# Float64 weights to float32 in three vector operations instead of four, early low parts on VectorE, early v read where it was loaded

## Chip, core and metric

The kernel runs on one core of a Trainium2 chip. The metric is the device time of one execution in microseconds (us). PE is TensorE, DVE VectorE, ACT ScalarE, POOL GpSimd and SP the engine whose queue issues the DMAs.

## What is computed

Banded attention feeds a gated two-layer network, and that feeds a second one; everything is float32, but the six weight matrices arrive as float64.

```
scores = q @ k.T / 8 - slope_h * distance        # 4 batches, 8 heads, 768 positions, 64 wide
a      = softmax(scores where key < n_global or 0 <= query - key < n_local)
x      = a @ v                                    # as [3072, 512]
h      = x @ w_in                                 # [512, 2048]
x2     = (h * clip(h + 3, 0, 6) / 6) @ w_out      # [2048, 512]
out    = ((x2 @ w1) * (x2 @ w2)) @ w3 @ w_out2    # 1024 wide inside
```

## The kernel before

**Matmuls.** Large products are made from operands in two parts: a high part, rounded to the matmul's shorter format by a ScalarE copy, and a low part, the rest. Each product is three matmuls (high by high, low by high, high by low), recorded by `mm3` (line 64). The 3072 tokens go in eight tiles of 384.

**Weights.** 72 pieces of [128, 512] float64 are brought in one after another (`w_issue`, SP, three buffers `st`). Each goes through `w_abs` (line 148, ACT: absolute value of the upper words), `w_f32` (lines 161, 163, 165, 167: four DVE operations that shift and join the two words' bits into a float32, tile `cvt`), and then `w_split`: high part on ACT (line 171), low part on POOL (line 172). `w_steps` deals this work out in ticks, four to a piece. In tick 1 the piece before is split and the first of the four operations stands; ticks 2 to 4 hold the other three, and tick 4 also `w_abs` of the next piece and the load of a later one.

**Attention.** 32 units (two heads, half of a batch's queries), of three blocks of 128 queries; a loop of 96 steps and three to drain runs over the blocks in a software pipeline. One step, s, holds the scores of block s (PE, line 424), its maximum (DVE, line 434) and exponential (ACT, line 443); the normalising of block s - 1 (two small DVE operations, lines 449 and 450, and a POOL multiplication, line 451); the transposes and copy of block s - 2 (PE line 459, ACT); and the product with v of block s - 3 (PE line 490), whose two parts ACT and DVE write as `xt` (lines 356 and 359). The score tiles have one buffer each, so that the next block's scores on PE wait for this block's maximum on DVE. The first eight units (`WHOLE`) use full float32 matmuls, and `prep_v` copies their v on ACT (line 347) from the loaded tile `rv` into `vh`.

**Where the weights meet it.** From step 4 on each step holds four ticks, thus one piece of weights: 16 pieces (half of w_in and w_out) are converted in about steps 5 to 20. From step 14 on the matmuls of the first network fill PE between the attention's. After the attention the other half of w_in and w_out (16 pieces) is wanted at once, dealt out by ticks after each 850 or 600 ns of matmul work; the remaining 40 pieces follow in the course of that stage.

**What sets the order.** Every engine runs its instructions in the order in which this program writes them down; nothing is reordered later. `psm` has three PSUM buffers for the products `h` and `x`; DVE (line 528) or ACT (line 582) must have read one before PE writes it again.

```
nc.vector.scalar_tensor_tensor(t, a, TINY, hi, ALU.is_ge, ALU.mult)                              # 161
nc.vector.tensor_scalar(au, tu, 5, 2, ALU.logical_shift_left, ALU.logical_shift_right)           # 163
nc.vector.scalar_tensor_tensor(au, lo, 29, au, ALU.logical_shift_right, ALU.bitwise_or)          # 165
nc.vector.scalar_tensor_tensor(tu, tu, 0xC0000000, au, ALU.bitwise_and, ALU.bitwise_or)          # 167
```

Of the kernel before, what the change touches and what calls it, by code (L numbers as in the profile page):

```python
# [20 lines left out]
# A float64's upper word, read as a float32, is at least this from 2**-126 on.  # L21
TINY = float.fromhex("0x1.2p-15")


class Filler:
    """Queued matmul work, run in pieces between the steps of something else."""
# [28 lines left out]
def mm3(nc, out, jobs, ns, every=4, hook=None, first=True, last=True):  # L55
    """out = (or out +=) sum of a.T @ b; each job holds ((a_hi, a_lo), (b_hi, b_lo)). The hook runs before the fourth
    from last."""
    n = len(jobs)
    done = 0
    for i, ((ah, al), (bh, bl)) in enumerate(jobs):  # L60
        if hook is not None and i == max(0, n - 4):
            hook()
        for j, (a, b) in enumerate(((ah, bh), (al, bh), (ah, bl))):
            nc.tensor.matmul(out, a, b, start=(first and i == 0 and j == 0), stop=(last and i == n - 1 and j == 2))  # L64
            done += 1
            if done % every == 0:
                yield every * ns
    if done % every:
        yield (done % every) * ns
# [3 lines left out]
def kernel(ctx: ExitStack, tc: tile.TileContext, q, k, v, n_global, n_local,  # L73
# [50 lines left out]
    def need(*keys):  # L124
        """Ends when what the keys stand for has been emitted."""
# [4 lines left out]
    def w_issue(src):  # L130
        """src: float64 bits (or float32) as [128, n] or [128, a, n / a]."""
# [11 lines left out]
    def w_abs(x):  # L143
# [4 lines left out]
        nc.scalar.activation(a, st.bitcast(F32).rearrange("p (c t) -> p c t", t=2)[:, :, 1], AF.Abs)  # L148
        return a

    def w_f32(x, a):
        """float32 of what was loaded: the upper 24 bits of a float64's significand."""
# [4 lines left out]
        lo = st.rearrange("p (c t) -> p c t", t=2)[:, :, 0]  # L157
        hi = st.bitcast(F32).rearrange("p (c t) -> p c t", t=2)[:, :, 1]
        t = cvp.tile([P, 512], F32, tag="cvt", name="cvt", bufs=2)
        au, tu = a.bitcast(U32), t.bitcast(U32)  # L160
        nc.vector.scalar_tensor_tensor(t, a, TINY, hi, ALU.is_ge, ALU.mult)  # L161
        yield t
        nc.vector.tensor_scalar(au, tu, 5, 2, ALU.logical_shift_left, ALU.logical_shift_right)  # L163
        yield t
        nc.vector.scalar_tensor_tensor(au, lo, 29, au, ALU.logical_shift_right, ALU.bitwise_or)  # L165
        yield t
        nc.vector.scalar_tensor_tensor(tu, tu, 0xC0000000, au, ALU.bitwise_and, ALU.bitwise_or)
        yield t

    def w_split(t, hi, lo):  # L170
        nc.scalar.activation(hi, t, AF.Copy)  # L171
        nc.gpsimd.tensor_tensor(lo, t, hi.bitcast(F32), ALU.subtract)  # L172

    def w_steps():
        """Splitting one, bringing the next to float32, loading a third, in four pieces."""
        while True:
# [20 lines left out]
            if conv is not None:  # L197
                next(conv)
            if wload and not wload[0][2]:
                wload[0][2].append(w_abs(wload[0][0]))  # L200
# [34 lines left out]
    def load_unit(i):  # L235
# [22 lines left out]
        vr = att.tile([P, 2 * HB, 2, D], F32, tag="rv", name="rv")  # L258
# [33 lines left out]
    def masks(mk):  # L292
        """What is added to q k / slope: minus the distance, or -BIG (and the rest) for a key that is not kept."""
# [29 lines left out]
    def out_of_band():  # L323
        """How many of the two counts' bounds (of the banded path) fail."""
# [11 lines left out]
    def new_prep(i):  # L336
        def two(tag, shape):
            return tuple(att.tile(shape, F32R, tag=tag + z, name=tag + z) for z in "hl")
        prep[i] = dict(q=two("q", [P, HB * P]), k=two("k", [P, 2 * HB, P]), v=two("v", [P, 2 * HB, 2 * D]))

    def prep_v(i):
        hf = units[i][1]
        nv = 2 * HB - 1 + hf
        r = raw[i][3].rearrange("p n j d -> p n (j d)")[:, :nv]
        vh, vl = (x[:, :nv] for x in prep[i]["v"])
        if i < WHOLE:
            nc.scalar.activation(vh.bitcast(F32), r, AF.Copy)
            return
# [121 lines left out]
    def a_pv(st):  # L470
# [3 lines left out]
        vh, vl = prep[i]["v"]  # L474
# [6 lines left out]
        for j in range(2):  # L481
            jobs = []
            for t in range(nk):
                a, al = (x[:, c0 + t, j * D:(j + 1) * D] for x in (vh, vl))
                if i < WHOLE:
                    jobs.append((a.bitcast(F32), ph[:, t, j, :].bitcast(F32)))
                else:
                    jobs += [(a, ph[:, t, j, :]), (al, ph[:, t, j, :]), (a, pl[:, t, j, :])]
# [19 lines left out]
    def parts(x, g):  # L508
        """The two parts of x, at the next call (or flush)."""
# [13 lines left out]
    def gate(h, g):  # L523
        """g = h * min(max(h + 3, 0), 6)."""
# [18 lines left out]
    def first(t, WI, f0):  # L543
        """h and g of one tile of tokens."""
# [8 lines left out]
    def second(t, WO, done, f0):  # L553
        """Sums of g's products with w_out, each given to done."""
# [122 lines left out]

    for f in range(FB):
# [13 lines left out]
    def gen_w34():  # L692
        """w3 @ w_out2, one block of 128 rows after another."""
# [39 lines left out]
    def step(gen, ns):  # L733
        """All of gen, with a pump and other work after each ns of it."""
# [87 lines left out]
def general_path(tc, ident, c3, nbits, slope, q, k, v, weights, out):  # L822
# [5 lines left out]
    with tc.tile_pool(name="gdr", bufs=1, space=DRAM) as dr:  # L828
# [4 lines left out]
        with tc.tile_pool(name="gc", bufs=1) as gc, tc.tile_pool(name="gw", bufs=2) as gw, \  # L833
# [6 lines left out]
            # float64 to float32, as long runs of any shape  # L840
# [22 lines left out]
            # the counts as float32: upper word * 2**32 + lower word without sign  # L863
# [11 lines left out]
            # distances and masks of each block of 128 queries  # L875
# [157 lines left out]
```

## Time and profile before

| | |
|---|---|
| median of 3 runs | 1286.88 us (1286.28 to 1287.11) |
| span of the profiled execution | 1286.8 us |
| PE busy | 1238.0 us, 96% |
| DVE busy | 611.0 us, 47% |
| ACT busy | 564.8 us, 44% |
| POOL busy | 466.5 us, 36% |
| mean granted TensorE clock | 0.982 of 2.4 GHz |

The profiled execution's span is its own time as far as it is given; it lies 0.1 us from the median, so nothing of size stands around it. The shares are averages over stages that have different limits, so the table by stages (rows 1 below) is to be read before it. Busy time of PE is modelled, since matmuls are pipelined.

### The profile page before, as it was taken

The numbers are of one execution on the slowest core, as the hardware profiler recorded it, in microseconds if no ns is written. First come the engines' busy times: TensorE is split into PE (matmuls) and PEld (weight loads), VectorE is DVE, ScalarE is ACT, GpSimd is POOL, SyncE is SP. The second block draws the span as 40 slices with busy tenths as digits, with TensorE's granted clock in tenths as the row PEclk, the third lists the DMA queues.
The fourth block names the chain that finished last, engine by engine and source line by source line (L and its number), as shares of the span: only waits on it lengthen the run. The fifth ranks groups of instructions, "written<-read, shape, count | busy, mean of one in ns | idle before, by whom it ended". The sixth has DMA issues, their size and how long they took to land. (4 is left out here: it accounts for less than half of the span.)

```text
span 1286.8 us, 20618 instructions
## 1 busy us (share of the span) xinstructions
PE 1238.0 (96%) x7512; PEld 1134.0 (88%) x7512; DVE 611.0 (47%) x1523; ACT 564.8 (44%) x1441; POOL 466.5 (36%) x417
## 2 busy tenths in 40 slices
PE   6789999999999999879999999999999999999997
PEld 4567898999898989769999999999899898998996
DVE  5998566666666664989644446731010010010100
ACT  6777566666666664445324234442222222222221
POOL 2555354444445352556203034554322222222210
PEclk9699999999999999989999999999999999999999
DMA  6662424242324302545444345433201001010000
GB/s 159 160 187 62 123 58 132 60 127 74 103 67 120 79 2 91 164 174 168 158 159 144 115 135 176 142 99 106 68 8 50 23 28 49 17 33 31 9 17 28
DMA packets 164624, 119.16 MB, mean 93 GB/s; under 512 B 109217, under 2 KB 154273, under 8 KB 164513
## 3 DMA queue, kind: packets, MB, share of 16 engines
q1 hardware_dynamic: 164224, 117.74, 31.0%
q8 instruction: 62, 1.02, 0.3%
q14 instruction: 50, 0.40, 0.1%
q10 hardware_dynamic: 288, 0.00, 0.0%
HBM read 87.30 MB, written 30.41 MB: 91 GB/s over the span
## 5 line engine op out<-in xcount | busy, mean ns | idle before, releaser
L793 DVE TENSOR_TENSOR abr<-abr,pb 128x384 f32<-128x384 f32 x64 | 35.5, 554 | 349.0 <-PE pb L64 349.0
L451 POOL TENSOR_TENSOR e<-e,su 128x512 f32<-128x512 f32 (+1 forms) x96 | 93.0, 969 | 167.1 <-DVE su L450 160.4
L528 DVE SCALAR_TENSOR_TENSOR t<-t,h 128x384 f32<-128x384 f32 x128 | 70.6, 551 | 114.4 <-ACT t L527 114.0
L443 ACT ACTIVATE e<-e,mx 128x256 f32<-128x256 f32 (+1 forms) x192 | 92.7, 488 | 58.9 <-DVE mx L434 58.5
L527 ACT ACTIVATE t<-h,c 128x384 f32<-128x384 f32 x128 | 73.3, 573 | 41.4 <-PE h L64 40.5
L172 POOL TENSOR_TENSOR wa<-cvt,wa 128x512 fp32r<-128x512 f32 x40 | 61.8, 1545 | 64.2 <-ACT wa L171 58.5
L490 PE MATMUL pv<-ph,vh 128*64 128x128 f32 x440 | 79.8, 260 | 4.5 <-DVE xt1l L359 4.0
L148 ACT ACTIVATE cva<-st 128x512 f32<-128x512 f32 x72 | 47.9, 666 | 68.6 <-DMA st<-in_moe_w_dram 48.6
L434 DVE CUSTOM_DVE_ANT_0 e<-s,base 128x256 f32<-128x256 f32 (+1 forms) x192 | 69.1, 397 | 12.0 <-PE s L424 10.9
L64 PE MATMUL h<-xt0h,wa 128*128 128x384 f32 x256 | 74.4, 357 | 0.0
L64 PE MATMUL h<-xt1h,r 128*128 128x384 f32 x256 | 67.3, 343 | 5.9 <-DVE t L528 3.1
L64 PE MATMUL h<-xt1h,wa 128*128 128x384 f32 x256 | 71.5, 349 | 1.4 <-DVE t L528 1.4
L165 DVE SCALAR_TENSOR_TENSOR cva<-st,cva 128x512 uint32<-128x512 uint32 x72 | 69.3, 963 | 1.4
L490 PEld LDWEIGHTS pv<-ph,vh 128*64 128x64 f32 x440 | 58.1, 144 | 11.2 <-issue 5.6
L64 PE MATMUL h<-xt0h,r 128*128 128x384 f32 x256 | 66.4, 340 | 0.4 <-DVE part L774 0.4
L161 DVE SCALAR_TENSOR_TENSOR cvt<-cva,st 128x512 f32<-128x512 f32 x72 | 58.2, 808 | 15.6 <-ACT cva L148 15.6
L64 PE MATMUL pa<-xt0h,wa 128*128 128x384 f32 x256 | 65.0, 334 | 0.0
L64 PE MATMUL pa<-xt1h,wa 128*128 128x384 f32 x256 | 65.0, 334 | 0.0
L64 PE MATMUL pb<-xt0h,wa 128*128 128x384 f32 x256 | 65.0, 334 | 0.0
L64 PE MATMUL pb<-xt1h,wa 128*128 128x384 f32 x256 | 64.9, 334 | 0.0
L350 POOL TENSOR_TENSOR vl<-rv,vh 128x640 fp32r<-128x640 f32 (+1 forms) x24 | 40.8, 1701 | 66.0 <-DVE su L449 66.0
L163 DVE TENSOR_SCALAR cva<-cvt 128x512 uint32<-128x512 uint32 x72 | 62.9, 874 | 1.5
(245 smaller groups left out, 3576.3 us busy)
## 6 DMA issues: line engine op xcount, KB each, us to landing
st<-in_moe_w_dram SPq DMA_DIRECT2D x32, 512.0 KB, 4.8
st<-in_moe_w_out_dram SPq DMA_DIRECT2D x24, 512.0 KB, 3.9
st<-in_moe_w_in_dram SPq DMA_DIRECT2D x16, 512.0 KB, 4.2
rq<-in_q_dram SPq DMA_DIRECT2D x64, 96.0 KB, 3.0
rv<-in_v_dram SPq DMA_DIRECT2D x64, 96.0 KB, 2.5
p<-r SPq DMA_DIRECT2D x32, 192.0 KB, 1.9
part<-p SPq DMA_DIRECT2D x32, 192.0 KB, 5.0
x2s<-part SPq DMA_DIRECT2D x32, 192.0 KB, 2.0
```

The costliest lines, as they stand in the source:

```text
L64: nc.tensor.matmul(out, a, b, start=(first and i == 0 and j == 0), stop=(last and i == n - 1 and j == 2))
L148: nc.scalar.activation(a, st.bitcast(F32).rearrange("p (c t) -> p c t", t=2)[:, :, 1], AF.Abs)
L161: nc.vector.scalar_tensor_tensor(t, a, TINY, hi, ALU.is_ge, ALU.mult)
L163: nc.vector.tensor_scalar(au, tu, 5, 2, ALU.logical_shift_left, ALU.logical_shift_right)
L165: nc.vector.scalar_tensor_tensor(au, lo, 29, au, ALU.logical_shift_right, ALU.bitwise_or)
L172: nc.gpsimd.tensor_tensor(lo, t, hi.bitcast(F32), ALU.subtract)
L434: nc.vector.tensor_tensor_reduce(e[:, j, :W], d["sc"][j][:, :W], bs, -slope[2 * hp + j], 3.0e38, ALU.add, ALU.min, mx[:, j:j + 1])
L443: nc.scalar.activation(e[:, j, :W], e[:, j, :W], AF.Exp, bias=mx[:, j:j + 1], scale=-1.0, accum_out=su[:, j:j + 1])
L451: nc.gpsimd.tensor_tensor(d["e"][:, :, :W], d["e"][:, :, :W], su.unsqueeze(2).to_broadcast([P, 2, W]), ALU.mult)
L490: nc.tensor.matmul(ps[:, j, :], a, b_, start=(z == 0), stop=(z == len(jobs) - 1))
L527: nc.scalar.activation(t, h, AF.Relu, bias=c3)
L528: nc.vector.scalar_tensor_tensor(t, t, 6.0, h, ALU.min, ALU.mult)
```

## The change

ScalarE no longer makes the absolute value of the upper words but multiplies them by 2**-112, which lowers the exponent to float32's range and keeps the sign. On DVE a shift left by 3, an OR with the lower word's upper bits and an OR with the sign remain: three operations for four, in ticks 1 to 3. While the attention is written down, the low part of a piece is taken on DVE instead of POOL (`early`). For the first eight units v is no longer copied: the matmuls with v read the loaded tile, and the loaded tiles of these units rotate over the buffers of `rv`, `vh` and `vl`. Comments were taken out as well, which shifts the line numbers by one to three.

```diff
-    def w_abs(x):
+    def w_down(x):
...
-        nc.scalar.activation(a, st.bitcast(F32).rearrange("p (c t) -> p c t", t=2)[:, :, 1], AF.Abs)
+        nc.scalar.activation(a, st.bitcast(F32).rearrange("p (c t) -> p c t", t=2)[:, :, 1], AF.Copy, scale=DOWN)
...
-        nc.vector.scalar_tensor_tensor(t, a, TINY, hi, ALU.is_ge, ALU.mult)
+        nc.vector.tensor_scalar(tu, au, 3, None, ALU.logical_shift_left)
         yield t
-        nc.vector.tensor_scalar(au, tu, 5, 2, ALU.logical_shift_left, ALU.logical_shift_right)
+        nc.vector.scalar_tensor_tensor(tu, low, 29, tu, ALU.logical_shift_right, ALU.bitwise_or)
         yield t
-        nc.vector.scalar_tensor_tensor(au, lo, 29, au, ALU.logical_shift_right, ALU.bitwise_or)
+        nc.vector.scalar_tensor_tensor(tu, au, 0x80000000, tu, ALU.bitwise_and, ALU.bitwise_or)
         yield t
-        nc.vector.scalar_tensor_tensor(tu, tu, 0xC0000000, au, ALU.bitwise_and, ALU.bitwise_or)
-        yield t
+
+    early = [True]
...
-        nc.gpsimd.tensor_tensor(lo, t, hi.bitcast(F32), ALU.subtract)
+        (nc.vector if early[0] else nc.gpsimd).tensor_tensor(lo, t, hi.bitcast(F32), ALU.subtract)
...
-            if conv is not None:
-                next(conv)
             if wload and not wload[0][2]:
-                wload[0][2].append(w_abs(wload[0][0]))
+                wload[0][2].append(w_down(wload[0][0]))
...
-        vr = att.tile([P, 2 * HB, 2, D], F32, tag="rv", name="rv")
+        vr = att.tile([P, 2 * HB, 2, D], F32, tag=("rv", "vh", "vl")[i % 3] if i < WHOLE else "rv", name="rv")
...
     def prep_v(i):
         hf = units[i][1]
+        if i < WHOLE:
+            return
...
-        if i < WHOLE:
-            nc.scalar.activation(vh.bitcast(F32), r, AF.Copy)
-            return
...
-                    jobs.append((a.bitcast(F32), ph[:, t, j, :].bitcast(F32)))
+                    jobs.append((raw[i][3][:, c0 + t, j, :], ph[:, t, j, :].bitcast(F32)))
...
+    early[0] = False
     for f in range(FB):
         queue(kchunk(w_in, FA + f), WIB[f], ("wi", FA + f))
```

PE's and SP's instructions keep their order row by row. The first place where another engine's order changes is DVE in the attention, about step 7: `cva` is what ACT made of the upper words, `st` the loaded piece, `wa` a weight's high or low part, `su` the sums of the softmax. Before:

```order
L161 SCALAR_TENSOR_TENSOR cvt<-cva,st 128x512
L163 TENSOR_SCALAR cva<-cvt 128x512
L165 SCALAR_TENSOR_TENSOR cva<-st,cva 128x512
L359 TENSOR_TENSOR xt0l<-pv_554,xt0h 64x128 x2
L167 SCALAR_TENSOR_TENSOR cvt<-cvt,cva 128x512
L449 TENSOR_SCALAR su<-su 128x2
L450 RECIPROCAL su<-su 128x2
```

And now, at the same place:

```order
L175 TENSOR_TENSOR wa_77<-cvt,wa_76 128x512
L164 TENSOR_SCALAR cvt<-cva 128x512
L166 SCALAR_TENSOR_TENSOR cvt<-st,cvt 128x512
L168 SCALAR_TENSOR_TENSOR cvt<-cva,cvt 128x512
L361 TENSOR_TENSOR xt0l<-pv_541,xt0h 64x128 x2
L451 TENSOR_SCALAR su<-su 128x2
L452 RECIPROCAL su<-su 128x2
```

One operation went and one came: the low part of the piece before now stands ahead of the shift, and `cvt` is complete before the two `xt` parts rather than behind them.

The second place is POOL in the same steps, where `e` is the softmax's numerator. Before:

```order
L451 TENSOR_TENSOR e<-e,su 128x2x128
L172 TENSOR_TENSOR wa_77<-cvt,wa_76 128x512
L451 TENSOR_TENSOR e<-e,su 128x512
L172 TENSOR_TENSOR wa_79<-cvt,wa_78 128x512
L451 TENSOR_TENSOR e<-e,su 128x512
L172 TENSOR_TENSOR wa_81<-cvt,wa_80 128x512
```

And now, with the matmuls' low parts `g0l` to `g2l` that begin at step 15:

```order
L453 TENSOR_TENSOR e<-e,su 128x512 x6
L516 TENSOR_TENSOR g0l<-t,g0h 128x384
L453 TENSOR_TENSOR e<-e,su 128x512
L516 TENSOR_TENSOR g1l<-t,g1h 128x384
L453 TENSOR_TENSOR e<-e,su 128x512
L516 TENSOR_TENSOR g2l<-t,g2h 128x384
```

All 16 low parts of weights left POOL here.

The third place is DVE behind the attention, in the first products with the second half of w_in, where `t` is what the gate makes of a product `h`. Before:

```order
L528 SCALAR_TENSOR_TENSOR t<-t,h 128x384
L167 SCALAR_TENSOR_TENSOR cvt<-cvt,cva 128x512
L161 SCALAR_TENSOR_TENSOR cvt<-cva,st 128x512
L528 SCALAR_TENSOR_TENSOR t<-t,h 128x384
L163 TENSOR_SCALAR cva<-cvt 128x512
L165 SCALAR_TENSOR_TENSOR cva<-st,cva 128x512
L528 SCALAR_TENSOR_TENSOR t<-t,h 128x384
L167 SCALAR_TENSOR_TENSOR cvt<-cvt,cva 128x512
```

And now:

```order
L530 SCALAR_TENSOR_TENSOR t<-t,h 128x384
L164 TENSOR_SCALAR cvt<-cva 128x512
L530 SCALAR_TENSOR_TENSOR t<-t,h 128x384
L166 SCALAR_TENSOR_TENSOR cvt<-st,cvt 128x512
L168 SCALAR_TENSOR_TENSOR cvt<-cva,cvt 128x512
L530 SCALAR_TENSOR_TENSOR t<-t,h 128x384
L164 TENSOR_SCALAR cvt<-cva 128x512
L166 SCALAR_TENSOR_TENSOR cvt<-st,cvt 128x512
```

Here an operation of each piece went and none came, so that fewer stand between one `t` and the next; the low parts stay on POOL.

## Rows read from the trace of the kernel before

**Rows 1.** Busy by stage: each engine's us (count), granted clock, DMA share, GB/s.

```profile
28.00:78.00 50.00, 39.14 (x173) 27.90 (x174) 48.57 (x114) 37.24 (x105) 23.64 (x18) 0.69 0.62 157
78.00:122.00 44.00, 39.86 (x236) 31.79 (x235) 42.01 (x97) 33.97 (x91) 28.18 (x23) 0.96 0.47 132
122.00:497.00 375.00, 375.00 (x2929) 337.79 (x2928) 235.75 (x831) 234.35 (x741) 160.22 (x147) 1.00 0.32 83
497.00:575.00 78.00, 62.81 (x319) 57.59 (x318) 64.83 (x81) 36.68 (x70) 41.66 (x32) 0.95 0.50 165
575.00:1287.00 712.00, 704.05 (x3781) 667.83 (x3780) 207.35 (x336) 207.39 (x392) 207.09 (x185) 1.00 0.25 80
```

**Rows 2.** What PE waited for, 28 to 126 us: total us, times, longest.

```profile
PE s L424 <- DVE mx L434: 10.2, 8, 2.2
PE pv L490 <- DVE xt1l L359: 4.0, 3, 1.9
```

**Rows 3.** The same, 504 to 575 us.

```profile
PE h L64 <- DVE t L528: 4.5, 7, 1.7
PE x L64 <- ACT r L171: 3.0, 1, 3.0
PE h L64 <- ACT r L582: 2.6, 1, 2.6
```

**Rows 4.** DVE in time, one attention step: start, us, instruction [idle before].

```profile
40.47 0.16 DVE L449 TENSOR_SCALAR su<-su 128x2 f32<-128x2 f32 x1
...
41.42 1.17 DVE L161 SCALAR_TENSOR_TENSOR cvt<-cva,st 128x512 f32<-128x512 f32 x1
42.62 1.39 DVE L163 TENSOR_SCALAR cva<-cvt 128x512 uint32<-128x512 uint32 x1
44.04 0.69 DVE L165 SCALAR_TENSOR_TENSOR cva<-st,cva 128x512 uint32<-128x512 uint32 x1
44.65 0.57 DVE L359 TENSOR_TENSOR xt0l<-pv,xt0h 64x128 fp32r<-64x128 f32 x2
45.26 0.69 DVE L167 SCALAR_TENSOR_TENSOR cvt<-cvt,cva 128x512 uint32<-128x512 uint32 x1
45.87 0.16 DVE L449 TENSOR_SCALAR su<-su 128x2 f32<-128x2 f32 x1
```

**Rows 5.** POOL in time, the same view; steps 6, 8 and 15.

```profile
30.64 1.04 POOL L451 TENSOR_TENSOR e<-e,su 128x512 f32<-128x512 f32 x1 [6.02 <-DVE su L450]
...
41.00 1.04 POOL L451 TENSOR_TENSOR e<-e,su 128x512 f32<-128x512 f32 x1 [2.67 <-DVE su L450]
42.00 1.73 POOL L172 TENSOR_TENSOR wa<-cvt,wa 128x512 fp32r<-128x512 f32 x1
...
78.35 1.04 POOL L451 TENSOR_TENSOR e<-e,su 128x512 f32<-128x512 f32 x1 [2.67 <-DVE su L450]
```

**Rows 6.** DVE in time, the first piece, while POOL is idle.

```profile
27.10 0.69 DVE L161 SCALAR_TENSOR_TENSOR cvt<-cva,st 128x512 f32<-128x512 f32 x1 [2.96 <-ACT cva L148]
27.82 0.43 DVE L163 TENSOR_SCALAR cva<-cvt 128x512 uint32<-128x512 uint32 x1
```

**Rows 7.** Copies of v, line 347: duration in ns, first and last start.

```profile
L347 ACT ACTIVATE vh<-rv x8: 720/782/846, 8.1 to 113.3; 128x640 f32<-128x640 f32 x4, 128x768 f32<-128x768 f32 x4
```

**Rows 8.** DVE groups, 504 to 575 us: busy us, mean ns, idle before.

```profile
L161 DVE SCALAR_TENSOR_TENSOR cvt<-cva,st 128x512 f32<-128x512 f32 x16 | 11.6, 726 | 0.0
```

**Rows 9.** DVE in time behind the attention, one piece.

```profile
531.29 0.69 DVE L161 SCALAR_TENSOR_TENSOR cvt<-cva,st 128x512 f32<-128x512 f32 x1
...
532.48 1.67 DVE L165 SCALAR_TENSOR_TENSOR cva<-st,cva 128x512 uint32<-128x512 uint32 x1
534.18 0.69 DVE L167 SCALAR_TENSOR_TENSOR cvt<-cvt,cva 128x512 uint32<-128x512 uint32 x1
534.79 0.68 DVE L161 SCALAR_TENSOR_TENSOR cvt<-cva,st 128x512 f32<-128x512 f32 x1
```

**Rows 10.** POOL in time, the same piece.

```profile
532.12 1.48 POOL L172 TENSOR_TENSOR r<-cvt,r 128x512 fp32r<-128x512 f32 x1 [2.02 <-ACT r L171]
```

More of the change, by code (lines that the diff above doesn't have):

```diff
@@ L22 @@
 TINY = float.fromhex("0x1.2p-15")
+DOWN = 2.0 ** -112
 class Filler:
@@ L156, in w_f32 @@
                 yield st.bitcast(F32)[:, :n]
-        lo = st.rearrange("p (c t) -> p c t", t=2)[:, :, 0]
-        hi = st.bitcast(F32).rearrange("p (c t) -> p c t", t=2)[:, :, 1]
+        low = st.rearrange("p (c t) -> p c t", t=2)[:, :, 0]
         t = cvp.tile([P, 512], F32, tag="cvt", name="cvt", bufs=2)
         au, tu = a.bitcast(U32), t.bitcast(U32)
-        nc.vector.scalar_tensor_tensor(t, a, TINY, hi, ALU.is_ge, ALU.mult)
+        nc.vector.tensor_scalar(tu, au, 3, None, ALU.logical_shift_left)
         yield t
-        nc.vector.tensor_scalar(au, tu, 5, 2, ALU.logical_shift_left, ALU.logical_shift_right)
+        nc.vector.scalar_tensor_tensor(tu, low, 29, tu, ALU.logical_shift_right, ALU.bitwise_or)
         yield t
-        nc.vector.scalar_tensor_tensor(au, lo, 29, au, ALU.logical_shift_right, ALU.bitwise_or)
+        nc.vector.scalar_tensor_tensor(tu, au, 0x80000000, tu, ALU.bitwise_and, ALU.bitwise_or)
         yield t
-        nc.vector.scalar_tensor_tensor(tu, tu, 0xC0000000, au, ALU.bitwise_and, ALU.bitwise_or)
-        yield t
+    early = [True]
     def w_split(t, hi, lo):
         nc.scalar.activation(hi, t, AF.Copy)
-        nc.gpsimd.tensor_tensor(lo, t, hi.bitcast(F32), ALU.subtract)
+        (nc.vector if early[0] else nc.gpsimd).tensor_tensor(lo, t, hi.bitcast(F32), ALU.subtract)
     def w_steps():
@@ L338, in two @@
             return tuple(att.tile(shape, F32R, tag=tag + z, name=tag + z) for z in "hl")
-        prep[i] = dict(q=two("q", [P, HB * P]), k=two("k", [P, 2 * HB, P]), v=two("v", [P, 2 * HB, 2 * D]))
+        prep[i] = dict(q=two("q", [P, HB * P]), k=two("k", [P, 2 * HB, P]))
+        if i >= WHOLE:
+            prep[i]["v"] = two("v", [P, 2 * HB, 2 * D])
     def prep_v(i):
         hf = units[i][1]
+        if i < WHOLE:
+            return
         nv = 2 * HB - 1 + hf
@@ L473, in a_pv @@
         nk, c0 = d["nk"], d["c0"]
-        vh, vl = prep[i]["v"]
+        vh, vl = prep[i].get("v", (None, None))
         ph, pl = d["p"]
@@ L483, in a_pv @@
             for t in range(nk):
-                a, al = (x[:, c0 + t, j * D:(j + 1) * D] for x in (vh, vl))
                 if i < WHOLE:
-                    jobs.append((a.bitcast(F32), ph[:, t, j, :].bitcast(F32)))
+                    jobs.append((raw[i][3][:, c0 + t, j, :], ph[:, t, j, :].bitcast(F32)))
                 else:
+                    a, al = (x[:, c0 + t, j * D:(j + 1) * D] for x in (vh, vl))
                     jobs += [(a, ph[:, t, j, :]), (al, ph[:, t, j, :]), (a, pl[:, t, j, :])]
```

## Prediction, made before the changed kernel was run

> **What bounds the kernel now.** I read the table by stages first [rows 1]. From 122 to 497 us PE is busy in all 375 us at clock 1.00, and behind 575 us in 704.05 of 712. What the change moves on other engines there is covered by PE, and I cost it at nothing. Three stages are left. From 28 to 78 us DVE is busy 48.57 of 50 us, while PE has only 39.14, and these at a mean granted clock of 0.69. From 78 to 122 us DVE has 42.01 of 44, PE 39.86. From 497 to 575 us DVE has 64.83 of 78, PE 62.81. So DVE sets the pace where weights are converted in a hurry. The waits say the same. In the attention PE's scores wait for the maximum on DVE, 10.2 us, and its product with v for DVE's `xt` part, 4.0 us [rows 2]; behind the attention it waits for the gate on DVE, for a weight's high part on ACT and for a product that ACT had yet to read [rows 3], and ACT stands behind the conversion that feeds it. What can be won is bounded by PE: 94 - 39.14 - 39.86 = 15.0 us of idle time up to 122 us, and 78 - 62.81 = 15.2 us later, plus what the half clock costs.
>
> **One step of the attention before.** From one normalising to the next are 40.47 to 45.87 us, 5.40 us [rows 4]. Its parts by start times: normalising and maximum 0.95, first operation 1.20, second 1.42, third 0.61, the `xt` parts 0.61, fourth 0.61. The first piece of all, with POOL idle, took 0.72 for the first and the second lasted 0.43 [rows 6]. So 1.4 us of the step is waiting for POOL. The second operation ends at 44.01, 0.28 us after POOL's low part of a weight (42.00 to 43.73); the first ends at 42.59, 0.55 after POOL's normalising (41.00 to 42.04) [rows 4, 5].
>
> **The same step after.** DVE's own work stays: a 0.69 operation goes, the low part comes. No row shows that low part with all operands in SBUF; its bounds are 0.43 (the operation with one tensor) and 0.69 (with two) [rows 6], and I take 0.69, as it reads two. It stands where the first operation stood and will wait for POOL's normalising like it: 1.20. Then nothing of POOL is left in its way: shift 0.46 (0.43 and the gap; 0.69 if a one-step shift were slower), OR with the lower word 0.72, sign 0.61, `xt` 0.61. The sum is 0.95 + 1.20 + 0.46 + 0.72 + 0.61 + 0.61 = 4.55, a gain of 0.85 us per step. Nine such steps lie between 30.64 and 78.35 us [rows 5]: 7.7 us; the first piece has one operation less, 0.6. From 78 to 122 us six more would give 5.1. But there PE is busy nine tenths of the time and can give back 4.1 us of idle and 0.04 x 39.86 = 1.6 of clock at most, and low parts of `g` on POOL still come in the way; I take 3.5.
>
> From this I take off 1.5 us for the clock. PE's work from 28 to 78 us is 39.14 x 0.69 = 27.0 us at 2.4 GHz and 54 at 1.2 GHz. A step's share of the 50 us is about a tenth, so 2.7 or 5.4 us against DVE's 4.55: wherever the clock stands at its lower level, PE and not DVE is next. Attention: 7.7 + 0.6 + 3.5 - 1.5 = **10.3 us**.
>
> Two sentences aside. The Trainium skill (SBUF — State Buffer, Who interferes with whom) says that VectorE and GpSimd share one pair of SBUF ports by an exclusive lock, and that who comes second is blocked until the first has finished. The rows agree nearly: after POOL's end the blocked operation took 0.55 us of its 0.69, and by a full lock the step would be 4.69 and the gain 1.3 us smaller in all.
>
> **Behind the attention.** A piece without a gate between takes 531.29 to 534.79, 3.50 us [rows 9]; the third operation starts 1.19 us in and lasts 1.67, as it meets POOL's low part (532.12 to 533.60) [rows 10]. Now the last of three operations starts 0.46 + 0.72 = 1.18 in, meets the same low part, ends at the same place, and the 0.61 of the fourth is gone. The gain per piece lies between this 0.61 and the 0.73 of an unhindered operation, of which there are 16 of mean 726 ns [rows 8]: 16 x 0.67 = **10.7 us**. The weights for the products `x` come that much earlier; PE's bound, 15.2 us of idle, is not reached.
>
> **What costs nothing.** The eight copies of v, 0.72 to 0.85 us each on ACT [rows 7], about 6 us: ACT has 37.24 of 50 us and 33.97 of 44 [rows 1], and nobody is shown waiting for one; without this cover they would be worth up to 5 us more. The scaling for the absolute value is the same pass over the same tile. POOL's 16 low parts go; POOL was not full.
>
> **New waits.** The low part on DVE waits for ACT's high part, and behind it queue the conversion, `xt`, the normalising and the next maximum, for which PE's scores wait. `cvt` is complete before the `xt` parts now: from there to the low part are 0.61 + 0.95 = 1.56 us, for one copy on ACT and, every third step, one for k ahead of it. The copy of 512 columns takes less than the 0.72 us of one of 640 [rows 7], so it fits with some 0.8 us to spare. On SP, the load of unit 9's v now waits for the last product of unit 6 with v, about three steps later than for the copy; behind it queue unit 10's loads, which are written down no earlier, and unit 9's v is wanted three steps after that. I cost it at nothing.
>
> **The sum.** The profiled span is 1286.8 us, the median 1286.88. 1286.8 - 10.3 - 10.7 = 1265.8, so 1266 us.
>
> **Rivals.**
> - *DVE's time in the attention was not POOL's doing*, or another wait on POOL takes its place. Then its work there, four operations for four, is what it was, and only the later stage gains: 1286.8 - 10.7 = 1276. Against it: the ends that lie 0.28 and 0.55 us behind POOL's [rows 4, 5].
> - *PE at 1.2 GHz from 28 to 78 us.* PE needs 54 us there instead of 50, gains 3.5 later: 1286.8 + 4 - 3.5 - 10.7 = 1277. For it: 0.69 is already a mean of both levels. Against it: a DVE with fewer delays gives PE less idle time. The Trainium skill (TensorE: Matmul & The Clock Gate, HAM oscillation — how this bites in real kernels) has gaps between matmuls throw the clock back to half, and gaps remain here; the rows show only that both levels occur.
> - *Slower: the lower clock also holds where the first network's matmuls fill PE.* Up to 122 us PE has 27.0 + 39.86 x 0.96 = 65.3 us of work at 2.4 GHz, 131 at 1.2, against 94: 1286.8 + 37 - 10.7 = 1313. It decides from 21 us of loss on, some 40 us of lower clock with PE always busy. Against it: 0.96 from 78 to 122 us.
> - *Nothing to speak of.* The low part waits for ACT by a whole 0.85 us each step, and behind the attention the pieces wait for their loads: 1287. Against it: there the DMA engines are busy half the time [rows 1].
> - *More.* The clock costs nothing, 78 to 122 us gives its full 5.1, the copies of v 1, and the shorter way from gate to gate also removes waits of DVE for ACT, so that PE's 15.2 us come back: 1286.8 - 8.3 - 6.1 - 15.2 = 1257.
>
> **How the numbers follow.** Forecast 0.70, more 0.08, POOL not the cause 0.09, lower clock to 78 us 0.05, nothing 0.04, slower 0.04. The forecast's own range, with the unknown low part (0.43 to 0.69, 16 times: 4 us), the full lock and the other ends, is about 1260 to 1272; to hold 8 in 10 I reach to 1257 and 1278. A difference of 0.2% is about what a measurement of this kernel can tell from no change. Faster by more: 0.70 + 0.08 + 0.09 + 0.05 = 0.92; within it 0.04; slower 0.04.
>
> **What would show it.** Right, if the shift lasts 0.43 us in the attention, the low part there about 1.2 at most and the others 0.7; if nine steps take some 40 us instead of 47.7; if the piece behind the attention takes 2.9 us; and if DVE stays over nine tenths busy to 78 us. Wrong, if the shift still lasts over 1 us, if PE is the full engine at 0.5 clock before 78 us, if DVE waits for ACT ahead of the low parts, or if the end behind the attention comes where it came, waiting for loads.

## The result and the profile after

| | before | after |
|---|---|---|
| median of the runs | 1286.95 us (1286.28 to 1287.11) | 1265.54 us (1263.40 to 1266.31) |
| span of the profiled execution | 1286.8 us | 1261.2 us (its time 1263.40 us) |
| ratio of the medians | 1 | 0.9831, 95% interval 0.9817 to 0.9845 |

The changed kernel is 21.4 us faster, 1.7%. The forecast was 1266. The two profiled spans differ by 25.6 us, more than the medians. In part that is because the profiled execution of after is the fastest of its four (the others have spans of 1262.8 to 1264.1). Most of the rest is on the other side: the listed runs of before have spans 1.8 us below their times, so its median would have a span of 1285.2, and the profiled one is 1.6 us longer. A lead read from the two traces can therefore be some 4 us too long by the end. So sizes are taken below from medians where a run gives them, and places from the traces.

The table by stages of the kernel after, with its columns (stretch, its length, then the us of PE, PEld, DVE, ACT and POOL with counts, PE's granted clock, DMA share, GB/s); it answers [rows 1], without the stage in the middle:

```profile
28.00:78.00 50.00, 42.10 (x222) 30.19 (x223) 48.11 (x136) 42.78 (x124) 11.79 (x12) 0.85 0.82 218
78.00:122.00 44.00, 44.00 (x280) 35.91 (x279) 34.66 (x102) 31.30 (x91) 19.14 (x17) 1.00 0.29 72
...
497.00:575.00 78.00, 68.62 (x368) 64.88 (x367) 66.45 (x80) 39.51 (x74) 48.47 (x36) 0.98 0.55 186
575.00:1261.00 686.00, 679.77 (x3654) 644.21 (x3652) 163.61 (x272) 196.20 (x373) 195.13 (x177) 1.00 0.24 77
```

Up to 78 us DVE still sets the pace, with 48.11 of 50 us. From 78 to 122 us PE is busy in all 44 us at clock 1.00. DVE's 34.66 us there don't mean that it has room: the changed kernel is ahead, so its window ends behind the conversions. Between the same two normalisings, of steps 15 and 22, the view shows for before and then for after:

```profile
78.35:121.33 42.98, 38.84 (x230) 31.02 (x229) 41.00 (x92) 33.20 (x89) 27.51 (x23) 0.96 0.47 131
```

```profile
69.06:106.62 37.56, 37.56 (x232) 30.07 (x230) 36.70 (x93) 31.20 (x86) 17.16 (x15) 1.00 0.45 131
```

PE is full, and DVE nearly (36.70 of 37.56 us). Behind the attention PE does 68.62 us of work in 78 instead of 62.81.

One step on DVE, in order of time (start, us, instruction), beside [rows 4]:

```profile
37.98 0.17 DVE L451 TENSOR_SCALAR su<-su 128x2 f32<-128x2 f32 x1
...
39.00 1.11 DVE L175 TENSOR_TENSOR wa<-cvt,wa 128x512 fp32r<-128x512 f32 x1
40.03 0.41 DVE L164 TENSOR_SCALAR cvt<-cva 128x512 uint32<-128x512 uint32 x1
40.48 0.69 DVE L166 SCALAR_TENSOR_TENSOR cvt<-st,cvt 128x512 uint32<-128x512 uint32 x1
41.20 0.69 DVE L168 SCALAR_TENSOR_TENSOR cvt<-cva,cvt 128x512 uint32<-128x512 uint32 x1
41.81 0.57 DVE L361 TENSOR_TENSOR xt0l<-pv,xt0h 64x128 fp32r<-64x128 f32 x2
42.40 0.17 DVE L451 TENSOR_SCALAR su<-su 128x2 f32<-128x2 f32 x1
```

From 37.98 to 42.40 are 4.42 us, before 5.40. POOL in time shows the normalisings of steps 6, 8 and 15 as in [rows 5], with no low part of a weight between them:

```profile
30.10 1.04 POOL L453 TENSOR_TENSOR e<-e,su 128x512 f32<-128x512 f32 x1 [5.34 <-DVE su L452]
...
38.52 1.04 POOL L453 TENSOR_TENSOR e<-e,su 128x512 f32<-128x512 f32 x1 [3.39 <-DVE su L452]
...
69.06 1.04 POOL L453 TENSOR_TENSOR e<-e,su 128x512 f32<-128x512 f32 x1 [3.40 <-DVE su L452]
```

Nine steps take 69.06 - 30.10 = 38.96 us instead of 47.71. The next two steps of the same trace show what the low part still waits for:

```profile
43.15 1.38 DVE L175 TENSOR_TENSOR wa<-cvt,wa 128x512 fp32r<-128x512 f32 x1
...
47.84 0.69 DVE L175 TENSOR_TENSOR wa<-cvt,wa 128x512 fp32r<-128x512 f32 x1
```

```profile
47.36 0.61 POOL L453 TENSOR_TENSOR e<-e,su 128x256 f32<-128x256 f32 x1 [3.38 <-DVE su L452]
```

In the first, DVE's maximum is 0.27 us shorter and the low part that much longer (1.38 for 1.11); the step is 4.42 us as before it. In the second, POOL's normalising takes 0.61 us instead of 1.04, the low part lasts 0.69, and the step is 51.36 - 47.36 = 4.00 us. So about 0.4 us of a step is still the wait for POOL's normalising.

Behind the attention, DVE in time again, to set beside [rows 9]; the bracket is idle time ahead of the instruction and what ended it:

```profile
512.80 0.42 DVE L164 TENSOR_SCALAR cvt<-cva 128x512 uint32<-128x512 uint32 x1
513.25 0.69 DVE L166 SCALAR_TENSOR_TENSOR cvt<-st,cvt 128x512 uint32<-128x512 uint32 x1
513.98 1.67 DVE L168 SCALAR_TENSOR_TENSOR cvt<-cva,cvt 128x512 uint32<-128x512 uint32 x1
515.57 0.41 DVE L164 TENSOR_SCALAR cvt<-cva 128x512 uint32<-128x512 uint32 x1
...
520.07 0.43 DVE L164 TENSOR_SCALAR cvt<-cva 128x512 uint32<-128x512 uint32 x1 [1.66 <-ACT cva L151]
```

POOL, ACT and SP's queue (SPq) beside it:

```profile
513.63 1.47 POOL L175 TENSOR_TENSOR r<-cvt,r 128x512 fp32r<-128x512 f32 x1 [2.02 <-ACT r L174]
519.31 0.66 ACT L151 ACTIVATE cva<-st 128x512 f32<-128x512 f32 x1 [2.99 <-DMA st<-in_moe_w_out_dram]
513.95 0.81 SPq L585 DMA_DIRECT2D p<-r  x2
514.87 0.88 SPq L142 DMA_DIRECT2D st<-in_moe_w_out_dram  x2
```

A piece takes 515.57 - 512.80 = 2.77 us instead of 3.50. The last operation meets POOL's low part and lasts 1.67 us, as the third of four did. The last row of DVE is new: DVE waits for ACT's scaling, which itself stands behind the load. And the load came late because of the order on SP. Its buffer was free at 512.15 us, when the OR of three pieces earlier ended, but SP issued it at 514.87, behind two stores of products (`p<-r`), for which SP had waited 5.9 us until ACT had copied them. These 2.7 us are more than DVE's wait of 1.66. No run moves the stores. PE's waits from 470 to 620 us (total us, times, longest), to set beside [rows 3]:

```profile
PE h L66 <- ACT r L584: 2.6, 1, 2.6
PE x L66 <- ACT r L174: 2.2, 1, 2.2
PE h L66 <- DVE t L530: 1.9, 4, 0.7
```

### The profile page after: what moved, and what is told of

Its sections match the earlier page's. It is cut to its first block, busy times and chain, and to the rows that moved or that the text cites. A ratio compares the mean times of both kernels' runs of the same rounds, so it can differ in the third digit from the quotient of the medians.

```text
span 1261.2 us, 20589 instructions
## 1 busy us (share of the span) xinstructions
PE 1227.0 (97%) x7512; PEld 1126.2 (89%) x7512; DVE 561.6 (45%) x1467; ACT 558.3 (44%) x1433; POOL 441.4 (35%) x401
## 3 DMA queue, kind: packets, MB, share of 16 engines
q8 instruction: 62, 1.02, 0.3%
## 5 line engine op out<-in xcount | busy, mean ns | idle before, releaser
L166 DVE SCALAR_TENSOR_TENSOR cvt<-st,cvt 128x512 uint32<-128x512 uint32 x72 | 72.4, 1005 | 1.5
L168 DVE SCALAR_TENSOR_TENSOR cvt<-cva,cvt 128x512 uint32<-128x512 uint32 x72 | 69.2, 960 | 1.4
L806 ACT ACTIVATE ot<-po 128x512 f32<-128x512 f32 x24 | 14.4, 599 | 108.0 <-PE po L66 77.4
L361 DVE TENSOR_TENSOR pl<-pt,ph 128x512 fp32r<-128x512 f32 (+1 forms) x72 | 46.4, 644 | 34.2 <-ACT ph L358 33.8
L795 ACT ACTIVATE abr<-pa 128x384 f32<-128x384 f32 x64 | 31.5, 492 | 65.9 <-PE pa L66 61.3
L461 PE MATMUL pt<-ident,e 128*128 128x128 f32 x352 | 57.2, 283 | 3.3 <-ACT ph L356 3.2
```

The lines of the kernel that those rows point to most:

```text
L166: nc.vector.scalar_tensor_tensor(tu, low, 29, tu, ALU.logical_shift_right, ALU.bitwise_or)
L168: nc.vector.scalar_tensor_tensor(tu, au, 0x80000000, tu, ALU.bitwise_and, ALU.bitwise_or)
L361: nc.vector.tensor_tensor(lo, src, hi.bitcast(F32), ALU.subtract)
L461: nc.tensor.transpose(ps[:, t, j, :], d["e"][:, j, t * P:(t + 1) * P], ident)
```

## Experiments

Each ratio is to the kernel before, run on the same chip: 1287.70 us for the first four kernels, 1286.98 for the next four, 1287.83 for the last four. The kernel after was run again with the last four, and gave 1264.47 us there.

### The three operations alone

Before, with the new conversion only; low parts stay on POOL and v is copied.

```
- nc.scalar.activation(a, st.bitcast(F32).rearrange("p (c t) -> p c t", t=2)[:, :, 1], AF.Abs)
+ nc.scalar.activation(a, st.bitcast(F32).rearrange("p (c t) -> p c t", t=2)[:, :, 1], AF.Copy, scale=DOWN)
...
- nc.vector.scalar_tensor_tensor(t, a, TINY, hi, ALU.is_ge, ALU.mult)
+ nc.vector.tensor_scalar(tu, au, 3, None, ALU.logical_shift_left)
  yield t
...
```

> The kernel before with the three-operation conversion alone: low parts stay on POOL, v is copied. If waiting for POOL is what stretches a step of the attention, the two-port shift will wait for POOL's normalising, and an OR for POOL's low part of the weight: a step of about 4.9 us (5.40 before, 4.42 in the changed kernel), 4 to 5 us gained by step 15, some 10 behind the attention, in all 1271 to 1274. The rival, that only the number of DVE operations counts, expects a step of 5.40 - 0.72 = 4.7 or shorter than in the changed kernel, since DVE has the low part no more to do: 1262 or less.

Measured: 1267.91 us (1267.04 to 1268.95), ratio 0.9853 (0.9836 to 0.9869), 19.8 us faster. DVE and POOL in one step:

```profile
43.70 1.17 DVE L162 TENSOR_SCALAR cvt<-cva 128x512 uint32<-128x512 uint32 x1
44.91 1.64 DVE L164 SCALAR_TENSOR_TENSOR cvt<-st,cvt 128x512 uint32<-128x512 uint32 x1
46.58 0.69 DVE L166 SCALAR_TENSOR_TENSOR cvt<-cva,cvt 128x512 uint32<-128x512 uint32 x1
```

```profile
44.55 1.45 POOL L171 TENSOR_TENSOR wa<-cvt,wa 128x512 fp32r<-128x512 f32 x1
```

The OR ends at 46.55, 0.55 us behind POOL's low part, so the wait for POOL is still there; a step takes 4.77 us, 0.63 less than before, which is the one operation that went. That step lies nearer to the rival's 4.7 than to my 4.9, so it doesn't part the two; the long OR beside POOL's low part does, and a step longer than the changed kernel's 4.42 though DVE has an operation less. The time was not as expected, by 3 us. What I had undersized is what the step is worth later: by step 22 this kernel is 121.33 - 110.10 = 11.2 us ahead, though the nine steps up to step 15 give only 5.6. From step 15 to 22 it takes 38.35 us, before 42.98 and the changed kernel 37.56, with PE nearly full (37.20 us), so that the low part can add little there. The three operations are thus the larger share of the gain: 19.8 us, where the changed kernel without the edit of v (below) has 22.6 on the same chip.

### The low parts on DVE alone

```
- nc.gpsimd.tensor_tensor(lo, t, hi.bitcast(F32), ALU.subtract)
+ (nc.vector if early[0] else nc.gpsimd).tensor_tensor(lo, t, hi.bitcast(F32), ALU.subtract)
```

> The kernel before with the early low parts on DVE alone: four operations, v copied. If POOL's low part was what the operations waited for, DVE has 0.69 us more to do and 0.7 to 0.9 less to wait: a step of 5.1 to 5.3 us, behind the attention nothing changes, 1282 to 1286. The rival, only the count: a step of 6.1 us, 16 x 0.7 us lost, 1297.

Measured: 1282.77 us (1281.47 to 1283.82), ratio 0.9963 (0.9949 to 0.9977), 4.9 us faster. DVE in time:

```profile
40.73 1.11 DVE L174 TENSOR_TENSOR wa<-cvt,wa 128x512 fp32r<-128x512 f32 x1
41.76 0.68 DVE L161 SCALAR_TENSOR_TENSOR cvt<-cva,st 128x512 f32<-128x512 f32 x1
42.48 0.43 DVE L163 TENSOR_SCALAR cva<-cvt 128x512 uint32<-128x512 uint32 x1
```

As expected, and the rival is out. DVE has an operation more per step and the step is still shorter, 5.04 us instead of 5.40 (from POOL's normalising at 40.25 to the next at 45.29): the shift falls from 1.39 us [rows 4] to 0.43. Together with the run before this makes a square of nine steps: 47.71 with neither edit, 42.07 with the three operations, 44.51 with the low parts, 38.96 with both. The gains of 5.6 and 3.2 add up to the 8.75 of both, to 0.1.

### v without a copy, alone and left out

Before, with v loaded into the place where the product reads it; and the kernel after with the eight copies put back.

```
- vr = att.tile([P, 2 * HB, 2, D], F32, tag="rv", name="rv")
+ vr = att.tile([P, 2 * HB, 2, D], F32, tag=("rv", "vh", "vl")[i % 3] if i < WHOLE else "rv", name="rv")
...
- if i < WHOLE:
-     nc.scalar.activation(vh.bitcast(F32), r, AF.Copy)
-     return
...
```

> The kernel before with v read where it was loaded, nothing else. If nobody waits for the eight copies: 1286 to 1287, steps of 5.40 as before. The rival, that ACT also limits the attention: up to 5 us faster, 1282; or slower, if the later load of unit 9's v holds somebody up.

> The changed kernel with the eight copies of v back. If they are covered also at the shorter step: 1265 to 1267, steps of 4.4. The rival: ACT with 42.8 of 50 us busy from 28 to 78 us in the changed kernel has no more room, and the copies show as 3 to 5 us: 1269 to 1271.

Measured: alone 1287.27 us (1285.88 to 1288.77), ratio 0.9997 (0.9987 to 1.0006); after without it 1265.14 us (1264.51 to 1266.93), ratio 0.9832 (0.9816 to 0.9848). No difference either way beyond the 2 us that these intervals leave, and with the copies ACT has 43.99 of the 50 us up to 78: the cover holds even there.

### POOL's passes put back, with nothing else

```
  (nc.vector if early[0] else nc.gpsimd).tensor_tensor(lo, t, hi.bitcast(F32), ALU.subtract)
+ if early[0]:
+     for c in (0, 160, 320):
+         z = cvp.tile([P, 160], F32, tag="scr", name="scr", bufs=1)
+         nc.gpsimd.tensor_tensor(z, t[:, c:c + 160], hi.bitcast(F32)[:, c:c + 160], ALU.subtract)
```

> The kernel after, with GpSimd computing the early low parts once more for nothing (in three pieces of 160 columns, into a small scratch tile; VectorE's own low parts are used as in the kernel after). This puts back the suspected cause alone: POOL's two-operand passes beside DVE's conversion, with all of DVE's operations as they are. Theory (DVE waits while POOL works): in the attention one or two of DVE's two-operand operations get longer by together 0.7 to 1.5 us; a step takes 5.1 to 5.9 us instead of 4.42, nine steps 45 to 52 us instead of 38.96, and the time is 1271 to 1281. Rival (only the number of DVE's own operations counts; POOL's presence does not): a step stays at 4.4, the time at 1264 to 1267.

Measured: 1271.96 us (1271.53 to 1272.66), ratio 0.9882 (0.9867 to 0.9897), by the ratios 6.6 to 8.1 us slower than the kernel after. DVE by groups from 28 to 78 us (busy us, mean ns, idle before); first this kernel, then the kernel after:

```profile
L166 DVE SCALAR_TENSOR_TENSOR cvt<-st,cvt 128x512 uint32<-128x512 uint32 x11 | 9.7, 879 | 0.4
L168 DVE SCALAR_TENSOR_TENSOR cvt<-cva,cvt 128x512 uint32<-128x512 uint32 x10 | 8.8, 877 | 0.3
L164 DVE TENSOR_SCALAR cvt<-cva 128x512 uint32<-128x512 uint32 x10 | 7.4, 744 | 0.0
```

```profile
L168 DVE SCALAR_TENSOR_TENSOR cvt<-cva,cvt 128x512 uint32<-128x512 uint32 x12 | 9.0, 749 | 0.4
L166 DVE SCALAR_TENSOR_TENSOR cvt<-st,cvt 128x512 uint32<-128x512 uint32 x12 | 8.3, 693 | 0.4
L164 DVE TENSOR_SCALAR cvt<-cva 128x512 uint32<-128x512 uint32 x11 | 4.6, 415 | 0.0
```

DVE does the same work in both, and each of its three conversion operations is longer with POOL beside it: the shift by 0.33 us in the mean, the OR by 0.19, the sign by 0.13. The idle time ahead of them is no longer than in the kernel after, so the time went by within the operations. Nine steps take 45.65 us. So POOL's presence by itself costs DVE time; the rival, that only the number of operations counts, is out. The 0.74 us per step are at the low end of what I expected; POOL's passes are shorter here than one of 512 columns, and each of several DVE operations loses a little where one lost much.

### The low parts behind the attention on DVE too

First at the place in the order where the kernel after has them, for the 16 pieces behind the attention as well:

```
- early = [True]
+ early = [32]
...
- (nc.vector if early[0] else nc.gpsimd).tensor_tensor(lo, t, hi.bitcast(F32), ALU.subtract)
+ early[0] -= 1
+ (nc.vector if early[0] >= 0 else nc.gpsimd).tensor_tensor(lo, t, hi.bitcast(F32), ALU.subtract)
```

> The kernel after, with the low parts of the 16 pieces behind the attention on VectorE too (where the third operation no longer meets one on GpSimd), at the place in the order where the kernel after issues them on GpSimd. Theory (behind the attention the engine that sets the pace is DVE, and POOL's low part costs it 0.9 to 1.0 us per piece, the 1.67 against 0.69 of the sign operation): a low part of DVE's own costs about the same, 0.69, and waits besides for ACT's high part of the same weight, some 0.4 to 0.8 us, since nothing of DVE's lies between the conversion and it there. So a piece takes 2.8 to 3.3 us, against 2.77 in the kernel after, and the time is 1264 to 1271. Rival (the loads set the pace there, since DVE already waits for ACT's scaling, 0.43 to 3.65 us before some pieces): another microsecond of DVE's changes nothing, 1264 to 1267. If it is faster by over 2 us, both are wrong.

Measured: 1264.67 us (1263.44 to 1265.53), ratio 0.9823 (0.9810 to 0.9836). DVE in time:

```profile
513.54 0.69 DVE L176 TENSOR_TENSOR r<-cvt,r 128x512 fp32r<-128x512 f32 x1 [0.70 <-ACT r L174]
514.15 0.42 DVE L164 TENSOR_SCALAR cvt<-cva 128x512 uint32<-128x512 uint32 x1
514.61 0.69 DVE L166 SCALAR_TENSOR_TENSOR cvt<-st,cvt 128x512 uint32<-128x512 uint32 x1
515.33 0.69 DVE L168 SCALAR_TENSOR_TENSOR cvt<-cva,cvt 128x512 uint32<-128x512 uint32 x1
516.72 0.69 DVE L176 TENSOR_TENSOR r<-cvt,r 128x512 fp32r<-128x512 f32 x1 [0.70 <-ACT r L174]
```

A piece takes 3.18 us, 0.4 more than in the kernel after, with the wait of 0.70 us for ACT's high part as expected. Yet the time is the same: from 490 to 560 us DVE no longer waits for ACT's scaling, for which the kernel after waits 3.3 us there in three places, and its waits for ACT's part of the gate fall from 6.5 to 0.9 us. The 8.1 us that it waits for ACT's high parts stand in their place. The time lies where both theories put it; the absent waits say that the loads, as SP issues them, take part in the pace of this stage.

Then with the low part one operation later, so that ACT's high part is ready: for the same 32 pieces, and for all that `w_split` makes. Those are not 72: 16 of the 72 pieces (of `w3`) are never split, so 56 weights have a low part, and the edit also moves the 40 low parts of tiles that are loaded as float32 behind the attention.

```
- (nc.vector if early[0] else nc.gpsimd).tensor_tensor(lo, t, hi.bitcast(F32), ALU.subtract)
+ early[0] -= 1
+ if early[0] < 0:
+     nc.gpsimd.tensor_tensor(lo, t, hi.bitcast(F32), ALU.subtract)
+     return None
+ return lambda: nc.vector.tensor_tensor(lo, t, hi.bitcast(F32), ALU.subtract)
...
  if conv is not None:
      next(conv)
+ if low is not None:
+     low()
+     queued.discard(done_key)
  yield
...
```

> As the run before, the low part on VectorE for the 32 pieces of the attention and behind it, but issued one operation later, behind the OR of the next weight, so that ACT's high part is ready. Theory (DVE's own work and POOL's lock set the pace of a piece): behind the attention a piece is 0.42 + 0.69 + 0.69 + 0.69 and gaps, 2.5 to 2.6 us against 2.77, 16 x 0.2 = 3 us less; in the attention the low part had only gaps of some 0.4 us to lose, since it lasted 1.11 of which 0.69 is its own if it was held up by POOL's normalising; the OR would then be held up instead, so that a step stays at 4.3 to 4.5. Together 1260 to 1264. Rival (loads set the pace behind the attention, and PE in the second half of the attention): 1264 to 1267.

> As the run before, with all 72 low parts on VectorE. Behind some 575 us PE is busy without a pause, so both theories expect what the run before gives, within 2 us; only the last weights of the 16 that the second network needs first could differ.

Measured: 1262.92 us (1261.62 to 1264.29), ratio 0.9808 (0.9795 to 0.9821), and for all of them 1262.67 us (1260.73 to 1263.25), ratio 0.9806 (0.9792 to 0.9819). Both medians lie in the theory's range and below the rival's, and they don't differ from each other. The last of these, beside the kernel after on one chip:

> The kernel after itself, for a comparison on one chip with the next: 1264 to 1267 by both theories.

> All low parts on VectorE, issued one operation later, once more. Theory (the lock costs as much as the operation itself, so DVE does not lose by doing the low parts): 1.5 to 3 us faster than the kernel after on the same chip, 1262 to 1264. Rival (the difference to the kernel after came from another chip): within 1 us of it.

Measured: after 1264.47 us (1263.58 to 1265.05), ratio 0.9819 (0.9805 to 0.9832); all of `w_split`'s low parts on DVE 1261.34 us (1261.22 to 1261.72), ratio 0.9797 (0.9784 to 0.9810). The five runs of each don't overlap: 3.1 us, a quarter of a percent, just over the 1.5 to 3 that I expected; another chip is not the cause. It is the fastest version here. Its DVE in time, a step of the attention and a piece behind it:

```profile
42.27 1.11 DVE L164 TENSOR_SCALAR cvt<-cva 128x512 uint32<-128x512 uint32 x1
43.42 0.69 DVE L166 SCALAR_TENSOR_TENSOR cvt<-st,cvt 128x512 uint32<-128x512 uint32 x1
44.03 0.68 DVE L179 TENSOR_TENSOR wa<-cvt,wa 128x512 fp32r<-128x512 f32 x1
44.63 0.69 DVE L168 SCALAR_TENSOR_TENSOR cvt<-cva,cvt 128x512 uint32<-128x512 uint32 x1
...
510.18 0.42 DVE L164 TENSOR_SCALAR cvt<-cva 128x512 uint32<-128x512 uint32 x1
...
512.45 0.42 DVE L164 TENSOR_SCALAR cvt<-cva 128x512 uint32<-128x512 uint32 x1
...
516.99 0.43 DVE L164 TENSOR_SCALAR cvt<-cva 128x512 uint32<-128x512 uint32 x1 [2.19 <-ACT cva L151]
```

The shift now takes over the wait for POOL's normalising, 1.11 us, and the step still falls from 4.42 to 4.30 us (from POOL's normalising at 42.06 to the next at 46.36; nine steps take 37.83 us instead of 38.96). The low part stands between two operations of which one reads the other's result: in the kernel after the start of the sign operation lies 0.72 us behind that of the OR, here 0.61 and 0.60 us lie between neighbours. The wait for POOL is not what differs: from the end of one normalising to the start of the next are 3.38 us in the kernel after (39.56 to 42.94) and 3.26 here (43.10 to 46.36). A piece behind the attention takes 512.45 - 510.18 = 2.27 us, where I expected 2.5 to 2.6, and waits for loads follow, 2.19 us at 516.99. There too SP issues the load (at 512.25 us) behind two stores that waited for ACT. My expectation for the step, 4.3 to 4.5 us, had no gain in it from the order.

### Each half of the gain by itself

The kernel after with the new work for the first 16 pieces alone, and from the 17th piece on alone.

```
+ def three(i):
+     count[i] += 1
+     return count[i] <= 16
...
+ if not three(1):
+     up = st.bitcast(F32).rearrange("p (c t) -> p c t", t=2)[:, :, 1]
+     nc.vector.scalar_tensor_tensor(t, a, TINY, up, ALU.is_ge, ALU.mult)
...
```

The second kernel has `count[i] > 16` there, and no low parts on DVE.

> The kernel after with the new conversion, the early low parts on VectorE and v without a copy for the first 16 pieces (in the attention) alone; from the 17th piece on ScalarE makes the absolute value again and VectorE the four operations of the kernel before. Theory (two separate gains, each with its own bound, that add up): only the attention's 14 us are left, since the pieces behind it take 3.5 us again, and the time is 1287 - 14 = 1271 to 1275. Rival (what the attention gains is given back by the pieces behind it, since they wait for loads; or those pieces gain nothing because the loads set their pace): 1264 to 1268 if the pieces behind it gain nothing from the new conversion, and 1280 or more if the attention's lead is lost.

> The other half: the first 16 pieces as in the kernel before (absolute value, four operations, low parts on GpSimd), the new three operations from the 17th piece on; v without a copy. Theory: the attention takes what it took before, 47.7 us for nine steps, and only the 10 us of the pieces behind it are gained, with at most 1.5 at the end: 1275 to 1278. Rival (the loads set the pace behind the attention): there the pieces wait for their loads, and less than 5 us are gained, 1282 to 1287. With the run before, the two gains should make 21 to 23 us; if they make much less or more, they hang on each other.

Measured: in the attention alone 1274.89 us (1273.48 to 1275.77), ratio 0.9898 (0.9883 to 0.9913), 12.9 us faster; behind it alone 1277.14 us (1276.93 to 1278.99), ratio 0.9923 (0.9909 to 0.9936), 10.7 us faster. Both lie in the theory's ranges. The sum is 23.6, a little over the 21 to 23 expected; the kernel after is 23.4 us faster on that chip. The first stage of the second kernel:

```profile
28.00:78.00 50.00, 44.56 (x166) 31.48 (x167) 48.59 (x117) 34.88 (x99) 23.90 (x19) 0.51 0.67 165
```

Each kernel works like after in its own half and like before in the other: nine steps take 69.13 - 30.18 = 38.95 us in the first and 77.72 - 30.04 = 47.68 in the second, a piece behind the attention 518.45 - 514.96 = 3.49 and 528.03 - 525.26 = 2.77. Only the second kernel's granted clock, 0.51, is like neither. What the attention gains is not given back: the first kernel starts the conversions of the second half 505.14 - 492.29 = 12.9 us earlier than before, and ends as much earlier.

## Why the prediction was right, point by point

**What bounds the kernel.** Right. An operation taken from DVE moved the end in both stages, and 16 pieces behind the attention gave what they were costed at. With POOL's low parts gone the shift fell from 1.39 us to 0.43, and POOL's passes put back slowed the kernel without any change to DVE's work: about 1.0 of the 1.4 us in each step was a wait for POOL's low part. The other 0.4, the wait for POOL's normalising, no run removed; that the step is 4.00 us where the normalising is 0.43 us shorter bears it out.

**The step.** Predicted 4.55 us, measured 4.42. By start times the parts are 1.02 (0.95), 1.03 for the low part (1.20), 0.45 (0.46), 0.72 (0.72), 0.61 (0.61) and 0.59 (0.61). Only the low part differs by more than 0.1: I had given it the way from start to start of the operation in whose place it stands. That one lasted 1.17 us and the next, which reads its result, began 0.03 behind its end; the low part lasted 1.11, since it began 0.06 later beside POOL, and the next, which doesn't read it, began 0.08 ahead of its end. The bound from the row that was nearest by place served better than those nearest by kind, 0.43 and 0.69, which were measured without POOL. Nine steps gave 8.75 us where 7.7 were predicted.

**From 78 to 122 us** is the term that was mis-sized. I took 3.5 us out of a bound of 5.7, for fear of the low parts of `g` on POOL. The lead of the changed kernel is 78.35 - 69.06 = 9.3 us at step 15 and 121.33 - 106.62 = 14.7 at step 22: 5.4 us, the bound nearly in full. Between those two steps PE went from 38.84 of 42.98 us to all of 37.56, at clock 1.00. POOL's low parts of `g` came in the way by no more than the 0.3 us that are left. DVE got little room by it (36.70 of 37.56 us; 35.19 of 38.87 in the second trace). Where the next engine is that nearly full, its bound is the value to take.

**The clock.** The 1.5 us that I took off didn't come: the granted clock from 28 to 78 us rose to 0.85, and was 0.83 to 0.86 in all five traces of this attention. The price of the lower clock was too high besides. I had multiplied PE's 39.14 busy us by the mean clock of 0.69 and doubled, 54 us. The kernel with the old attention and a granted clock of 0.51, which is the lower level nearly throughout, has PE busy in 44.56 of 50 us, and its nine steps still take 47.7 us. So busy time and mean clock of a stretch don't make a product: for nearly the same matmuls 39.14 x 0.69 is 27.0 and 44.56 x 0.51 is 22.7. That the mean also takes in PE's idle time is the likely reason, not shown. By that row a step of 5.30 us (47.7 / 9) holds 44.56 / 50 x 5.30 = 4.7 us of PE at the lower level: hidden there, and 0.4 us too much for the 4.33 of the changed kernel (38.96 / 9). So an estimate of the rival's price is some 3.5 us for nine steps. No run has this attention at the lower level throughout, so the rival's mechanism is not shown; its condition did not occur. What decides the clock stays open: the two kernels with the old attention and v without a copy had 0.67 and 0.51.

**The attention in all** gave 12.9 us by the medians (attention alone), where 10.3 were predicted, so the term was 2.6 us too small. By the trace of after it is 14.7, and the terms just named, 1.05 + 1.9 + 1.5, make up the 4.4 us; that execution was the fastest of four and before's profiled one was long, and in the second trace of the same kernel the lead at step 22 is 121.33 - 107.29 = 14.0 us.

**Behind the attention.** Predicted 10.7, measured 10.7 (behind alone). The piece gave 3.50 - 2.77 = 0.73 us, the upper end of what I took, and 16 of them 11.7. The trace of that kernel has 1.6 us of new waits for ACT's scaling in these pieces. I had waits for loads only in the rival of no gain; they are the likely place of the missing 1.0, and they come from SP's order of stores and loads shown above, which the prediction didn't look at for this stage: in this trace SP issues the load behind the longest of them at 527.33 us, after two stores, while its buffer was free at 524.61. The versions with these low parts on DVE show how near the limit lies: with 3.18 us a piece the time is the same, and with 2.27 DVE waits 2.19 us for one load.

**Costed at nothing.** v without a copy is worth nothing that the runs could show, alone or with the rest, as costed. The new wait of DVE for ACT's high part is 0.4 us in all up to 78 us. Behind 575 us little was gained or lost: attention alone is 579.50 - 566.51 = 13.0 us ahead at the first `part<-x` and 12.8 at the end of the trace, the changed kernel 579.50 - 555.27 = 24.2 us and 25.6.

**The sum.** 21.0 us were predicted; the changed kernel was 21.4 us faster in the first comparison and 23.4 in the second. So the sum of the terms was 0.4 to 2.4 us too small, and the hit to half a microsecond is partly luck: the attention's term was 2.6 us too small, and the first comparison came out 2 us below the second. Ahead of the prediction stands that nothing of size lies around the span, since 1286.8 and the median nearly agree; the runs list some 1.8 us between span and time for before and 2.2 in the first comparison for after, and the two figures agree only because the profiled execution was a long one.

**The rule on the ports.** The Trainium skill (SBUF — State Buffer, Who interferes with whom) has the second of VectorE and GpSimd blocked until the first is done. By that the step of 4.42 us would have been 0.14 longer (my 4.69 stood on a step of 4.55). The trace shows the order of events that the Trainium skill has: the low part, from 39.00 to 40.11, ends 0.55 us behind POOL's normalising (38.52 + 1.04). But 0.14 us of its 0.69 had gone by when POOL's record ends. The shift beside POOL's normalising ends 0.28 us behind it, with the same 0.14 of its 0.42 gone by (42.27 + 1.11 against 42.06 + 1.04 in the fastest version). Whether that is work done or POOL's recorded end coming late, the traces can't tell, and the sum by rows needs no answer.

## What to carry to other kernels

- Where a shared neighbour delays an engine that sets the pace, it can be right to give that engine more work: here a low part of 0.69 us on DVE itself replaced a delay by POOL, and the step fell by 0.36 us.
- Cost a step by the start times of its rows, with waits in the places where they are now, and take the next engine's bound for a stretch in which that engine is nearly full already.
- Compare two kernels between the same two events, not between the same two times: DVE's 34.66 of 44 us looked like room, and were 36.70 of 37.56 between the same steps.
- A half of a change, switched by a counter, tells what each stage gives; adding the halves (12.9 + 10.7 against 23.4) shows that neither takes from the other beyond the noise of a microsecond or two.

## What the runs showed that was not expected

- In these traces a DVE operation that reads what the one ahead of it wrote starts 0.72 us behind it, one that doesn't 0.61 (512 columns, two tensors). An independent operation put between two dependent ones shortened the step by some 0.12 us with the same work.
- A load that DVE waited for was held up on SP, by stores ahead of it that waited for ACT: 2.7 us between the free buffer and the issue.
- One POOL pass of 512 columns lengthened one DVE operation by 1.67 - 0.69 = 0.98 us. Three of 160 columns lengthened three operations by 0.33, 0.19 and 0.13 in the mean.
- PE at a granted clock of 0.51 instead of 0.69 for 50 us cost nothing where DVE set the pace: 47.7 us for nine steps at both.
